# Attention scores in pairs of adjacent PSUM banks: one exponential for two heads, and two of a step's three row maxima by one instruction

## The chip, the cores and the metric

The kernel runs on one core of one Trainium2 chip. The metric is the time of one execution on the device in microseconds (us). The engines are named as in the profile: PE is TensorE (matmuls; PEld are its weight loads), DVE is VectorE, ACT is ScalarE, POOL is GpSimd and SP is SyncE, which issues the DMAs. PSUM, the memory that PE writes its sums to, has eight banks; one bank holds 512 float32 numbers in each of 128 partitions.

## What is computed

Two attention blocks read the same input x of 2048 rows and 448 columns, and a gate mixes their results. Both blocks have 16 heads of 28 columns. Block A is local: each row looks at 8 rows at a distance of 2. Block B is full attention, and its 2048 x 2048 scores for each head are most of the work.

```python
def _B_ref(x, wqkv, wo):
    ...
    q, k, v = qkv[0], qkv[1], qkv[2]
    scores = jnp.einsum("bhqd,bhkd->bhqk", q, k) * (Dh ** -0.5)
    p = _softmax(scores, axis=-1)
    o = jnp.einsum("bhqk,bhkd->bhqd", p, v)
    return (lambda x, *d: x.transpose(*d))(o, 0, 2, 1, 3).reshape(B, S, D) @ wo

x = A_x
g = _sigmoid((x * gate_w).sum(-1, keepdims=True))
a = _A_ref(x, A_wqkv, A_wo)
b = _B_ref(x, B_wqkv, B_wo)
return g * a + (1 - g) * b
```

## The kernel before

All products are taken in two parts: a number is split into a high part and a low remainder, and a product is the sum of high x high, low x high and high x low. So a score block needs three matmuls (0, 1 and 2 below).

**PSUM.** Four single banks `R[0]` to `R[3]` (L52) stand for the whole kernel. The other four are first one tile `T[0]` of four banks (L60), and after the projections three single banks `T[0]` to `T[2]` (L445) and one for the weighted sums, `av` (L443).

**Projections, about the first 284 us.** A list of 92 tiles is worked through: 28 tiles of queries and keys (`qk_tile`, L244), 16 of values (`v_tile`, L262) and 48 for block A (`a_tile`, L268). Each tile is 11 matmuls into one bank (`project`, L241), and the banks rotate over `R[0]` to `R[3]` (`next_bank`). Then the bank is read. The first 11 tiles are read twice, by an ACT copy (L248, the high part) and by a DVE subtraction (L254, the low part). The later query and key tiles are read by two ACT copies (L248, L251) and subtracted on POOL. The tiles of values and of block A are read by one ACT copy (L265, L275). From the twelfth tile on, a *quad* follows each tile: four matmuls of the *first pass* (L121) into the four banks of `T[0]`, and one DVE maximum over all four (L125). The first pass computes scores with the high parts alone, to get the row maxima that the softmax subtracts later. It has 1024 blocks in all, and 80 quads take 320 of them.

**The step loop.** Block B is 16 units (four groups of four heads, times four blocks of 512 queries) of 16 steps each; a step `kt` takes 128 keys for four heads. In a step, `scores` (L862) issues 12 score matmuls (L882), three for each of four heads, and four exponentials on ACT (L885), one for each head's bank. In the order of PE stand also three blocks of the first pass, for units that come later: s0, s1 and s2, each a matmul (L121) with its own DVE maximum (L125). The order is written out in the string `WITH`: "10" is head 1, part 0; a head's exponential follows its part 2. After the scores come four products with the values (L851, `do_av`) for the step *before*. The 704 blocks that the quads leave last for 235 steps, so the last 21 steps run without s0 to s2, in the order `ALONE`. The seven banks rotate (L888-889): what a step's scores, exponentials and maxima free is handed out in a fixed order to the next step. Block A's work, and the steps by which a finished unit is scaled and stored, lie between, on POOL, DVE and ACT, where a small planner puts them: it counts a step as 2.3 us and a maximum as 0.607 us of DVE, and issues block A's instructions for DVE while its count is not behind.

**The output projection.** It starts in the last 21 steps. Seven of its instructions are issued after a step's products (`op_some`, L911). Row block j collects in one of two banks, `accs[j % 2]`, by matmuls at L693; then ACT copies the bank out (`op_out`, L701, for j up to 7; `op_part`, L809, for j = 8 to 11). `side["t"]` and `side["f"]` are banks for transposes. After the last step, j = 8 to 11 get their last products in four banks and a DVE addition each (`op_rest`, L814), and j = 12 to 15 are computed in the four banks of `order`.

Of the kernel before, what the change touches and what calls it, by code (L numbers as in the profile page):

```python
# [8 lines left out]
F32 = mybir.dt.float32  # L9
F32R = mybir.dt.float32r  # L10
AF = mybir.ActivationFunctionType
# [8 lines left out]
SCALE = DH ** -0.5  # L20
# [5 lines left out]
def gated_mix_kernel(ctx: ExitStack, tc: tile.TileContext, xT, xn, gw, wA, wB, woAB, out):  # L26
    nc = tc.nc
# [18 lines left out]
    pp = ctx.enter_context(tc.tile_pool(name="pp", bufs=16))  # L46
# [25 lines left out]
    KH = [cp.tile([128, S], F32R, name=f"KH{i}") for i in range(2)]  # L72
    KL = [cp.tile([128, S], F32R, name="KL0")]
# [4 lines left out]
    def init_kh(t):  # L78
        nc.gpsimd.memset(t.bitcast(F32), 1.0)

    def ptile(name):
        return pp.tile([128, 512], F32, tag="P", name=name)

    def dma_r(dst, src):
        nc.sync.dma_start(dst.bitcast(F32), src.bitcast(F32))  # L85
# [29 lines left out]
    def s1_mm(n, bank):  # L115
        u, i = divmod(n, 64)
        qs, kc, h = i // 16, i // 4 % 4, i % 4
        if i == 0 and u + 1 < NU:
            qhis[u + 1] = load_part(u + 1, "qhi", qk_hi)
        r = slice(32 * h, 32 * h + DH)  # L120
        nc.tensor.matmul(bank, qhis[u][r, 128 * qs:128 * qs + 128],  # L121
                         KH[u // NB % 3][r, 512 * kc:512 * kc + 512], start=True, stop=True)

    def s1_max(n, k, bank):
        nc.vector.tensor_reduce(MX[:, n % NMX:n % NMX + k], bank, axis=X, op=ALU.max)  # L125
        if n // 64 != (n + k) // 64:
            finished.append(n // 64)
        s1c[0] = n + k
# [28 lines left out]
            nc.sync.dma_start(nm[u].bitcast(F32)[:, 32 * a:32 * a + 32], r[32 * a:32 * a + 32, :])  # L157


    t0 = ptile("t0")  # L160
    nc.vector.memset(t0, 0.0)
    nc.vector.memset(zt, 0.0)
    nc.vector.memset(omg, 0.0)
# [2 lines left out]
    with tc.tile_pool(name="xp", bufs=1) as xp, tc.tile_pool(name="wp", bufs=2) as wp:  # L166
# [57 lines left out]

        banks4 = R
        pn = [0]
# [93 lines left out]
        r, t = xst[:, 0, 0:3, :], xst[:, 0, 3, :]  # L320
# [40 lines left out]
        for n, t in enumerate(tiles):  # L361
# [37 lines left out]
            if parts:  # L399
                u, t = parts.pop(0)  # L400
# [165 lines left out]
    for c in range(8):  # L566
# [20 lines left out]
        n = 0  # L587
# [10 lines left out]
    late = {"pool": 0.0, "dve": 0.0}  # L598
# [181 lines left out]
    for u in range(NU - 1):  # L780
        f = NJ * (u + 1)
# [72 lines left out]

    WITH = "10 20 s0 11 21 00 30 12 22 31 01 s1 32 02 s2".split()
    ALONE = "00 10 20 30 01 11 21 31 02 12 22 32".split()
    held = {}
    order = R + T  # L860

    def scores(u, kt, cur):  # L862
        g = u // NB
        n = s1c[0]
        k = min(3, s1e - n)
        qh, ql = Qs[u]
        ks = slice(128 * kt, 128 * kt + 128)
        free = list(order)
        for tok in WITH if k else ALONE:
            if tok[0] == "s":  # L870
                i = int(tok[1])
                held[tok] = free.pop(0)
# [7 lines left out]
            if t == 0:  # L880
                held[a] = free.pop(0)
            nc.tensor.matmul(held[a], (KH[g % 3], KH[g % 3], KL[g % 2])[t][r, ks], (qh, ql, qh)[t][r, :], start=(t == 0), stop=(t == 2))  # L882
            if t == 2:
                p = ptile("P")
                nc.scalar.activation(p, held[a], AF.Exp, scale=SCALE)  # L885
# [25 lines left out]
    for u in range(NU):  # L911
        g, b = divmod(u, NB)
        for kt in range(NJ):
            st = NJ * u + kt
            now[0] = st
            if kt == 12 and u + 1 < NU:
                load_q(u + 1)
            run("pre", st)
            issue("sp", st, 0)
            if st >= A_START:  # L920
                issue("pool", st, 4.2)
            if not adone and not any(lists.values()) and st > stored[0]:
                a_done(st)
            cur = {}
            left = s1e - s1c[0]
            for a in scores(u, kt, cur):
                if a == 2:
                    run("mid", st)
            run("dve", st)
            if u and kt == 6:  # L930
                late["dve"] += 0.25
            if finished:
                v = finished.pop(0)
                t = max_parts(v)
# [39 lines left out]
    for j in range(12, 16):  # L974
# [4 lines left out]
        bank = acc[j - 12]  # L979
# [40 lines left out]
```

## Time and profile before

| what | value |
|---|---|
| time, median of 3 runs | 959.87 us (958.42 to 961.14) |
| the profiled execution, its own time | 962.09 us |
| its span in the profile | 960.3 us |
| granted TensorE clock | 0.996 |
| PE busy | 947.0 us (99%) |
| DVE busy | 746.2 us (78%) |
| ACT busy | 647.7 us (67%) |
| POOL busy | 521.9 us (54%) |

In rows of the timeline the first number is the start in us from the start of the span, the second the length; then engine, line of the kernel, operation, output and input with their shapes, and how many such instructions the row joins. In brackets stands how long the engine was idle before, and what ended it. In rows of groups the numbers behind the first bar are the busy time in us and the mean length of one in ns, and behind the second the idle time before them.

### The profile page before, as it was taken

How to read it: one execution, taken by the hardware profiler on the slowest of the kernel's cores; microseconds unless marked ns; L12 is line 12 of the kernel's file. 1: busy time of each engine (PE TensorE's matmuls, PEld its weight loads, DVE VectorE, ACT ScalarE, POOL GpSimd, SP SyncE). 2: the span in 40 equal slices, each digit the busy share in tenths (PEclk: the TensorE clock that was granted, in tenths of full speed). 3: DMA queues.
4: the chain of work that ended last, by engine and by line, in shares of the span. 5: the costliest groups of instructions: out<-in, count | busy, mean ns of one | idle time of the engine just before them, and what ended most of it. 6: DMA issues, size and time to landing. Idle time of an engine off the chain costs nothing.

```text
span 960.3 us, 19993 instructions
## 1 busy us (share of the span) xinstructions
PE 947.0 (99%) x7578; PEld 553.0 (58%) x7578; DVE 746.2 (78%) x1166; ACT 647.7 (67%) x1309; POOL 521.9 (54%) x384
## 2 busy tenths in 40 slices
PE   8999999999999999999999999999999999999988
PEld 6766777777764544445444444444444444465657
DVE  6477888887779999999999999999998888400012
ACT  4434212122139999999999999999999999856541
POOL 1346101010018689999999999999993853100000
PEclk9999999999999999999999999999999999999999
DMA  9868414354246241314515331520312123344332
GB/s 277 284 199 251 137 48 126 108 135 127 77 117 212 67 126 50 89 47 118 157 42 124 108 88 37 167 72 22 107 43 51 33 68 111 111 141 127 110 102 90
DMA packets 102392, 108.15 MB, mean 113 GB/s; under 512 B 60844, under 2 KB 72636, under 8 KB 101400
## 3 DMA queue, kind: packets, MB, share of 16 engines
q1 hardware_dynamic: 102152, 106.62, 38.4%
q8 instruction: 59, 0.97, 0.4%
q10 hardware_dynamic: 144, 0.26, 0.1%
q14 instruction: 37, 0.30, 0.1%
HBM read 65.89 MB, written 40.48 MB: 111 GB/s over the span
## 4 chain that ended last, share of the span: by engine, by line
PE 87%; DMA 5%; DVE 3%; POOL 2%; SPq 1%; ACT 1%; issue 1%; ACTq 0%; DVEq 0%
PE av L851 25%; PE r L241 19%; PE r L882 15%; PE T L882 11%; PE T L121 6%; PE r L693 4%; PE T L693 4%; PE r L121 3%; DVE MX L125 2%; DMA kt<-a_scr 1%; DMA oal<-oa_scr 1%; PE r L671 1%; SPq L85 1%; POOL prod L541 1%; POOL oat L546 1%
## 5 line engine op out<-in xcount | busy, mean ns | idle before, releaser
L125 DVE TENSOR_REDUCE MX<-T 128x1 f32<-128x512 f32 (+1 forms) x384 | 384.6, 1021 | 59.6 <-PE T L121 54.5
L885 ACT ACTIVATE P<-r 128x512 f32<-128x512 f32 x581 | 329.8, 609 | 53.6 <-PE r L882 32.5
L125 DVE TENSOR_REDUCE MX<-r 128x1 f32<-128x512 f32 x400 | 262.5, 686 | 22.4 <-PE r L121 16.5
L851 PE MATMUL av<-P,V 128*32 128x512 f32 x2048 | 273.6, 606 | 0.4 <-ACT osb L708 0.4
L885 ACT ACTIVATE P<-T 128x512 f32<-128x512 f32 x443 | 255.7, 610 | 19.8 <-PE r L882 11.1
L121 PE MATMUL T<-KH,qhi 28*128 28x512 f32 x624 | 169.9, 475 | 0.9 <-DVE MX L125 0.6
L882 PE MATMUL r<-QH,KH 30*128 30x512 f32 x581 | 166.5, 471 | 1.2 <-ACT ast L275 0.6
L121 PE MATMUL r<-KH,qhi 28*128 28x512 f32 x400 | 162.6, 455 | 0.0
L882 PEld LDWEIGHTS r<-QH,KH 30*128 30x128 f32 x581 | 75.4, 183 | 125.5 <-DVE MX L125 111.3
L882 PE MATMUL T<-QH,KH 30*128 30x512 f32 x443 | 146.2, 472 | 1.0 <-ACT P L885 0.5
L882 PE MATMUL r<-QL,KH 28*128 28x512 f32 x581 | 141.8, 394 | 0.0
L882 PE MATMUL r<-QH,KL 28*128 28x512 f32 x581 | 141.4, 392 | 0.0
L491 POOL TENSOR_TENSOR prod<-qt,kt 128x896 f32<-128x896 f32 x64 | 135.0, 2114 | 7.1 <-DMA kt<-a_scr 7.0
L882 PE MATMUL T<-QL,KH 28*128 28x512 f32 x443 | 120.6, 395 | 0.0
L882 PE MATMUL T<-QH,KL 28*128 28x512 f32 x443 | 119.9, 392 | 0.0
L546 POOL TENSOR_TENSOR oat<-oat,prod 128x896 f32<-128x896 f32 x56 | 118.1, 2110 | 2.4
L882 PEld LDWEIGHTS T<-QH,KH 30*128 30x128 f32 x443 | 59.8, 182 | 91.5 <-DVE MX L125 86.5
L275 ACT ACTIVATE ast<-r 128x448 f32<-128x448 f32 x48 | 26.1, 545 | 106.7 <-PE r L241 102.3
L541 POOL TENSOR_TENSOR prod<-vt,L 128x896 f32<-128x896 f32 x56 | 95.5, 1705 | 0.7
L121 PEld LDWEIGHTS T<-KH,qhi 28*128 28x128 f32 x624 | 70.9, 182 | 35.9 <-DVE MX L125 27.6
L851 PEld LDWEIGHTS av<-P,V 128*32 128x32 f32 x2048 | 40.3, 108 | 67.6 <-issue 62.1
L681 DVE TENSOR_TENSOR oalo<-r,oah 128x384 fp32r<-128x384 f32 x16 | 8.9, 558 | 90.3 <-ACT onhi L680 80.6
(127 smaller groups left out, 1438.8 us busy)
## 6 DMA issues: line engine op xcount, KB each, us to landing
a_scr<-ast SPq DMA_DIRECT2D x24, 448.0 KB
qk_hi<-qkh SPq DMA_DIRECT2D x24, 256.0 KB
qk_lo<-qkl SPq DMA_DIRECT2D x24, 256.0 KB
rbc<-rs SPq DMA_DIRECT2D x60, 64.0 KB
KH<-qk_hi SPq DMA_DIRECT2D x16, 224.0 KB
qhi<-qk_hi SPq DMA_DIRECT2D x64, 56.0 KB
xg<-in_xn SPq DMA_DIRECT2D x16, 224.0 KB
KL<-qk_lo SPq DMA_DIRECT2D x16, 224.0 KB
```

Of the source, the lines that this page charges most:

```text
L85: nc.sync.dma_start(dst.bitcast(F32), src.bitcast(F32))
L121: nc.tensor.matmul(bank, qhis[u][r, 128 * qs:128 * qs + 128], KH[u // NB % 3][r, 512 * kc:512 * kc + 512], start=True, stop=True)
L125: nc.vector.tensor_reduce(MX[:, n % NMX:n % NMX + k], bank, axis=X, op=ALU.max)
L241: nc.tensor.matmul(bank, wa if wfirst else xa, xa if wfirst else wa, start=(i == 0), stop=(i == len(ORDER) - 1))
L275: nc.scalar.activation(stage[0][:, :, j % 2, :], bank[:, :D].rearrange("p (c e) -> p c e", e=56), AF.Copy)
L491: nc.gpsimd.tensor_tensor(out=p, in0=qt[c], in1=kvt["k", c % 2][:, HALO - DIL * w:HALO - DIL * w + NJ, :], op=ALU.mult)
L541: nc.gpsimd.tensor_tensor(out=dst.rearrange("p j (h d) -> p j h d", d=DH), in0=kvt["v", c % 2][:, HALO - DIL * w:HALO - DIL * w + NJ, :].r ...
L546: nc.gpsimd.tensor_tensor(out=oat[c], in0=oat[c], in1=oat[c, w], op=ALU.add)
L693: nc.tensor.matmul(bank[:, :D], src, wo[c][:, k, :], start=(first and k == ks[0] and i == 0), stop=(last and k == ks[-1] and i == 2))
L851: nc.tensor.matmul(av[32 * h:32 * h + 32, :], V[:, kt, 4 * g + h, :], tiles_[h], start=(kt == 0), stop=(kt == NJ - 1), skip_group_check=True)
L882: nc.tensor.matmul(held[a], (KH[g % 3], KH[g % 3], KL[g % 2])[t][r, ks], (qh, ql, qh)[t][r, :], start=(t == 0), stop=(t == 2))
L885: nc.scalar.activation(p, held[a], AF.Exp, scale=SCALE)
```

## The change

- `R` is no longer four tiles of one bank but the halves of two tiles of two adjacent banks, `RP[0]` and `RP[1]`. `R[0]` and `R[1]` are the halves of `RP[0]`, `R[2]` and `R[3]` those of `RP[1]`. The projections still rotate over `R[0]` to `R[3]`.
- The three banks `T` become one tile of two banks, `T[0]`, and one single bank, `T[1]`.
- In a step, heads "1" and "2" are always in `RP[0]`, and heads "3" and "0" in a pair that alternates from step to step between `RP[1]` and `T[0]` (`mine`); s1 and s2 go to the other one of these two (`other`), s0 to `T[1]`.
- An exponential covers a pair, 1024 columns: one follows "22", one follows "02". The maximum of s0 is taken alone, those of s1 and s2 by one instruction over a pair.
- The orders `WITH` and `ALONE` are changed to suit: s1 and s2 now stand last.
- The tiles for exponentials and other buffers in SBUF come from a pool of 8 pairs instead of 16 singles; single buffers are handed out as halves.
- The planner counts a step as 2.25 us and a maximum as 0.58 us.
- In the output projection, the two banks of `accs` are the halves of one pair, `side["f"]` is the second of them, `side["t"]` is `T[1]`, and `order` is the two halves of `RP[0]` and those of the remaining pair.

```diff
-    R = [ps.tile([128, 512], F32, name=f"r{i}") for i in range(4)]
+    RP = [ps.tile([128, 2, 512], F32, name=f"r{i}") for i in range(2)]
+    R = [t[:, i, :] for t in RP for i in range(2)]
...
-    banks([(), (), ()], ctx)
+    banks([(2,), ()], ctx)
...
     def s1_close():
-        order[:] = [held[x] for x in "0123"]
-        rest = [t for t in T + R if all(t is not o for o in order)]
-        accs.extend(rest[0:2])
-        side["f"], side["t"] = rest[1:3]
+        accs.extend(sums(1 - turn[0]))
+        side["f"], side["t"] = accs[1], T[1]
+        order.extend([RP[0][:, 0, :], RP[0][:, 1, :], *sums(turn[0])])
...
-    WITH = "10 20 s0 11 21 00 30 12 22 31 01 s1 32 02 s2".split()
+    WITH = "10 20 s0 11 21 30 00 12 22 31 01 32 02 s1 s2".split()
...
+        mine, other = ((RP[1], T[0]) if turn[0] == 0 else (T[0], RP[1]))
+        if k:
+            turn[0] = 1 - turn[0]
+        bank = {"1": RP[0][:, 0, :], "2": RP[0][:, 1, :], "3": mine[:, 0, :], "0": mine[:, 1, :],
+                "s0": T[1], "s1": other[:, 0, :], "s2": other[:, 1, :]}
...
                 if i < k:
-                    s1_mm(n + i, held[tok])
-                    s1_max(n + i, 1, held[tok])
+                    s1_mm(n + i, bank[tok])
+                if i == 0:
+                    s1_max(n, 1, T[1])
+                elif i == 2 and k > 1:
+                    s1_max(n + 1, k - 1, other[:, 0:k - 1, :])
...
-            if t == 2:
-                p = ptile("P")
-                nc.scalar.activation(p, held[a], AF.Exp, scale=SCALE)
-                cur[h] = p
+            if t == 2 and a in "20":
+                p = pair("P")
+                nc.scalar.activation(p, RP[0] if a == "2" else mine, AF.Exp, scale=SCALE)
+                cur[(h + 3) % 4], cur[h] = p[:, 0, :], p[:, 1, :]
                 yield len(cur)
-        if k:
-            order[:] = [held[x] for x in ("s0", "1", "s1", "2", "s2", "3", "0")]
...
-            step = 2.3 if left else 2.1
-            late["dve"] = max(0.0, late["dve"] + 0.607 * min(3, left) - step)
+            step = 2.25 if left else 2.1
+            late["dve"] = max(0.0, late["dve"] + 0.58 * min(3, left) - step)
```

The instructions of the engines are in program order, and a row in brackets waits for the engine that it names; instructions of one kind that follow one another are joined. First PE in the projections, at tiles of block A. Before, `r_128` to `r_131` are the four single banks, `T_0` is the tile of the quads, and L241 are a tile's 11 matmuls:

```order
L241 MATMUL r_129<-wh_1333,xh_175 128x448 [waits Activation_49]
L241 MATMUL r_129<-wh_1333,xh_175 128x448 x3
L241 MATMUL r_129<-wl_1334,xh_175 128x448 x4
L241 MATMUL r_129<-wh_1333,xl_179 128x448 x3
L121 MATMUL T_0_135<-KH_146,qhi 128x512 [waits DVE_49]
L121 MATMUL T_0_135<-KH_146,qhi 128x512 x3
L241 MATMUL r_130<-wh_1333,xh_175 128x448 [waits Activation_49]
L241 MATMUL r_130<-wh_1333,xh_175 128x448 x3
L241 MATMUL r_130<-wl_1334,xh_175 128x448 x4
L241 MATMUL r_130<-wh_1333,xl_179 128x448 x3
```

After, at the same place, `r_128` and `r_129` are the two pairs, and these are the two halves of `r_129` (lines are shifted: L241 is now L250, L121 is L130):

```order
L250 MATMUL r_129<-wh_1622,xh_171 128x448 x4
L250 MATMUL r_129<-wl_1623,xh_171 128x448 x4
L250 MATMUL r_129<-wh_1622,xl_175 128x448 x3
L130 MATMUL T_0_133<-KH_145,qhi 128x512 [waits DVE_49]
L130 MATMUL T_0_133<-KH_145,qhi 128x512 x3
L250 MATMUL r_129<-wh_1622,xh_171 128x448 [waits Activation_49]
L250 MATMUL r_129<-wh_1622,xh_171 128x448 x3
L250 MATMUL r_129<-wl_1623,xh_171 128x448 x4
L250 MATMUL r_129<-wh_1622,xl_175 128x448 x3
```

Before, every tile's first matmul waits for the ACT copy that last read its bank, which is that of four tiles earlier. After, a tile in a first half has no wait of its own, and a tile in a second half waits for the copy of the tile just ahead of it, in the first half of the same pair: the wait goes by the tile of PSUM, and the pair is now one.

Second, PE at the turn from one step to the next. Before, from s1 to the next step's "30" (L882 are scores, L121 s0 to s2, L851 the products with the values):

```order
L121 MATMUL r_131<-KH_147,qhi 128x512 [waits Activation_49]
L882 MATMUL r_129<-QH,KL_148 128x512
L882 MATMUL r_130<-QH,KL_148 128x512
L121 MATMUL r_128<-KH_147,qhi 128x512 [waits Activation_49]
L851 MATMUL av<-P,V 32x512 x4
L882 MATMUL T_2_2299<-QH,KH_146 128x512 [waits DVE_49]
L882 MATMUL T_0_2297<-QH,KH_146 128x512 [waits Activation_49]
L121 MATMUL r_131<-KH_147,qhi 128x512 [waits DVE_49]
L882 MATMUL T_2_2299<-QL,KH_146 128x512
L882 MATMUL T_0_2297<-QL,KH_146 128x512
L882 MATMUL T_1_2298<-QH,KH_146 128x512 [waits Activation_49]
L882 MATMUL r_128<-QH,KH_146 128x512 [waits DVE_49]
```

After, from s1 to the next step's "22" (`r_128` is `RP[0]`, `r_129` is `RP[1]`, `T_0` the other pair, `T_1` the bank of s0; L898 are scores, L130 s0 to s2, L859 the products):

```order
L130 MATMUL T_0_2239<-KH_2244,qhi 128x512 [waits Activation_49]
L130 MATMUL T_0_2239<-KH_2244,qhi 128x512
L859 MATMUL av<-P,V 32x512 x4
L898 MATMUL r_128<-QH,KH_145 128x512 [waits Activation_49]
L898 MATMUL r_128<-QH,KH_145 128x512
L130 MATMUL T_1_2240<-KH_2244,qhi 128x512 [waits DVE_49]
L898 MATMUL r_128<-QL,KH_145 128x512 x2
L898 MATMUL T_0_2239<-QH,KH_145 128x512 [waits DVE_49]
L898 MATMUL T_0_2239<-QH,KH_145 128x512
L898 MATMUL r_128<-QH,KL_2245 128x512 x2
```

Before, s1 and s2 each wait for one exponential of the step before, and "30" for the maximum of s2 of the step before. After, s1 waits for the exponential of the whole pair in which the step before had heads "3" and "0", and "30" and "00" for the one maximum over s1 and s2 in that same pair.

Third, PE in the output projection, where row block j = 0 ends and j = 1 begins (L693, now L702). Before:

```order
L693 MATMUL T_2_2299<-wo_10261,onhi_10791 128x448 [waits DMAHW6_49]
L693 MATMUL T_2_2299<-wo_10262,onhi_10791 128x448 [waits Pool_49]
L693 MATMUL T_2_2299<-wo_10261,onlo_10792 128x448 [waits DMAHW7_49]
L693 MATMUL r_128<-wo_10261,oah 128x448 [waits Activation_49]
L693 MATMUL r_128<-wo_10262,oah 128x448
```

After:

```order
L702 MATMUL r_129<-wo_9117,onhi_9572 128x448 [waits DMAHW6_49]
L702 MATMUL r_129<-wo_9118,onhi_9572 128x448 [waits Pool_49]
L702 MATMUL r_129<-wo_9117,onlo_9573 128x448 [waits DMAHW7_49]
L702 MATMUL r_129<-wo_9117,oah 128x448 [waits Activation_49]
L702 MATMUL r_129<-wo_9118,oah 128x448
```

Before, the two row blocks are in different tiles, and the wait of j = 1 is for an earlier reader of its own bank and for its input; after, both are in `r_129`, and j = 1 waits for the ACT copy that reads j = 0.

More of the change, by code (lines that the diff above doesn't have):

```diff
@@ L45, in gated_mix_kernel @@
     sp = ctx.enter_context(tc.tile_pool(name="sp", bufs=2))
-    pp = ctx.enter_context(tc.tile_pool(name="pp", bufs=16))
+    pp = ctx.enter_context(tc.tile_pool(name="pp", bufs=8))
     ps = ctx.enter_context(tc.tile_pool(name="ps", bufs=1, space=bass.MemoryType.PSUM))
-    R = [ps.tile([128, 512], F32, name=f"r{i}") for i in range(4)]
+    RP = [ps.tile([128, 2, 512], F32, name=f"r{i}") for i in range(2)]
+    R = [t[:, i, :] for t in RP for i in range(2)]
     tctx = [ExitStack()]
@@ L79, in init_kh, with pair @@
         nc.gpsimd.memset(t.bitcast(F32), 1.0)
+    def pair(name):
+        return pp.tile([128, 2, 512], F32, tag="P", name=name)
+    half = []
     def ptile(name):
-        return pp.tile([128, 512], F32, tag="P", name=name)
+        if not half:
+            t = pair(name)
+            half.extend((t[:, 1, :], t[:, 0, :]))
+        return half.pop()
     def dma_r(dst, src):
@@ L157, in max_store @@
             nc.sync.dma_start(nm[u].bitcast(F32)[:, 32 * a:32 * a + 32], r[32 * a:32 * a + 32, :])
-    t0 = ptile("t0")
+    t0 = pair("t0")[:, 0, :]
     nc.vector.memset(t0, 0.0)
@@ L852, in do_av, with sums @@
                              start=(kt == 0), stop=(kt == NJ - 1), skip_group_check=True)
-    WITH = "10 20 s0 11 21 00 30 12 22 31 01 s1 32 02 s2".split()
-    ALONE = "00 10 20 30 01 11 21 31 02 12 22 32".split()
-    held = {}
-    order = R + T
+    WITH = "10 20 s0 11 21 30 00 12 22 31 01 32 02 s1 s2".split()
+    ALONE = "10 20 30 00 11 21 31 01 12 22 32 02".split()
+    turn = [0]
+    order = []
+    def sums(i):
+        t = T[0] if i else RP[1]
+        return t[:, 0, :], t[:, 1, :]
     def scores(u, kt, cur):
@@ L867, in scores @@
         ks = slice(128 * kt, 128 * kt + 128)
-        free = list(order)
+        mine, other = ((RP[1], T[0]) if turn[0] == 0 else (T[0], RP[1]))
[3 more added lines that the diff above has]
+                "s0": T[1], "s1": other[:, 0, :], "s2": other[:, 1, :]}
         for tok in WITH if k else ALONE:
@@ L871, in scores @@
                 i = int(tok[1])
-                held[tok] = free.pop(0)
                 if i < k:
-                    s1_mm(n + i, held[tok])
-                    s1_max(n + i, 1, held[tok])
+                    s1_mm(n + i, bank[tok])
[3 more added lines that the diff above has]
+                    s1_max(n + 1, k - 1, other[:, 0:k - 1, :])
                 continue
@@ L879, in scores @@
             r = slice(32 * h, 32 * h + (DH + 2 if t == 0 else DH))
-            if t == 0:
-                held[a] = free.pop(0)
-            nc.tensor.matmul(held[a], (KH[g % 3], KH[g % 3], KL[g % 2])[t][r, ks], (qh, ql, qh)[t][r, :], start=(t == 0), stop=(t == 2))
-            if t == 2:
-                p = ptile("P")
-                nc.scalar.activation(p, held[a], AF.Exp, scale=SCALE)
-                cur[h] = p
+            nc.tensor.matmul(bank[a], (KH[g % 3], KH[g % 3], KL[g % 2])[t][r, ks], (qh, ql, qh)[t][r, :], start=(t == 0), stop=(t == 2))
+            if t == 2 and a in "20":
+                p = pair("P")
+                nc.scalar.activation(p, RP[0] if a == "2" else mine, AF.Exp, scale=SCALE)
+                cur[(h + 3) % 4], cur[h] = p[:, 0, :], p[:, 1, :]
                 yield len(cur)
-        if k:
-            order[:] = [held[x] for x in ("s0", "1", "s1", "2", "s2", "3", "0")]
     opj = [0]
```

## Prediction

> **What bounds the kernel now.** I read the page first (which engine is busy), then the busy time by stretches, then the timeline of one stretch in each stage, because a busy PE says nothing about which loop sets its pace.
>
> ```profile
> PE 947.0 (99%) x7578; PEld 553.0 (58%) x7578; DVE 746.2 (78%) x1166; ACT 647.7 (67%) x1309; POOL 521.9 (54%) x384
> 322.00:692.00 370.00, 369.51 (x3677) 179.18 (x3669) 357.41 (x693) 341.28 (x683) 352.75 (x240) 1.00 0.33 91
> ```
>
> The second line is a stretch of the step loop; its columns after the length are PE, PEld, DVE, ACT and POOL. PE is filled, but DVE (357.41 of 370) and ACT (341.28) are nearly so too. Hence no engine has much room, and what a step takes is set by the loops between them. The step length comes from the copies of `av`, one in each unit of 16 steps:
>
> ```profile
> 730.42 0.66 ACT L708 ACTIVATE osb<-av 128x512 f32<-128x512 f32 x1
> 767.33 0.63 ACT L708 ACTIVATE osb<-av 128x512 f32<-128x512 f32 x1
> ```
>
> 36.91 / 16 = 2.307 us a step. The loop that gives it stands in one step of the timeline (L882 scores, L885 exponentials, the L121 load is s2, L851 the products):
>
> ```profile
> 734.51 0.50 PE L882 MATMUL r<-QH,KH 30*128 30x512 f32 x2
> ...
> 735.11 1.32 DVE L125 TENSOR_REDUCE MX<-r 128x1 f32<-128x512 f32 x2 [0.46 <-PE r L121]
> ...
> 735.57 1.08 ACT L885 ACTIVATE P<-r 128x512 f32<-128x512 f32 x2 [0.32 <-PE T L882]
> ...
> 736.34 0.68 DVE L125 TENSOR_REDUCE MX<-T 128x1 f32<-128x512 f32 x1
> 736.54 1.10 ACT L885 ACTIVATE P<-T 128x512 f32<-128x512 f32 x2
> ...
> 737.08 0.18 PEld L882 LDWEIGHTS T<-QH,KH 30*128 30x128 f32 x1
> ...
> 737.69 0.18 PEld L121 LDWEIGHTS T<-KH,qhi 28*128 28x128 f32 x1
> ...
> 737.78 1.08 ACT L885 ACTIVATE P<-r 128x512 f32<-128x512 f32 x2
> ...
> 738.11 0.16 PEld L851 LDWEIGHTS av<-P,V 128*32 128x32 f32 x8 [0.24 <-issue]
> ...
> 739.10 0.18 PEld L882 LDWEIGHTS r<-QH,KH 30*128 30x128 f32 x2 [0.84 <-DVE MX L125]
> ```
>
> A step starts at 734.51. Its first exponential starts 1.06 later and the fourth ends at 736.54 + 1.10 = 737.64, 2.07 after the first began. The *next* step's s2 needs the bank of that fourth exponential and loads at 737.69, 0.05 later. The products start 0.42 behind it, and the step after that 0.99 later, at 739.10. So two steps take 1.06 + 2.07 + 0.05 + 0.42 + 0.99 = 4.59, or 2.295 each: this loop from PE over ACT to PE makes the 2.307. DVE holds "30" the same way: the third maximum ends at 737.02 and the load of "30" is at 737.08.
>
> **Part 1: exponentials and maxima in pairs.** The prices of the wider instructions come from shapes that are there:
>
> ```profile
> L125 DVE TENSOR_REDUCE MX<-r 128x1 f32<-128x512 f32 x400 | 262.5, 686 | 22.4 <-PE r L121 16.5 <-PE r L882 3.0 <-PE T L882 1.6
> L125 DVE TENSOR_REDUCE MX<-T 128x4 f32<-128x2048 f32 x80 | 183.3, 2292 | 45.0 <-PE T L121 44.1
> L275 ACT ACTIVATE ast<-r 128x448 f32<-128x448 f32 x48 | 26.1, 545 | 106.7 <-PE r L241 102.3 <-issue 4.4
> L248 ACT ACTIVATE qkh<-r 128x512 fp32r<-128x512 f32 x28 | 16.7, 597 | 44.5 <-PE r L241 44.5
> L885 ACT ACTIVATE P<-r 128x512 f32<-128x512 f32 x581 | 329.8, 609 | 53.6 <-PE r L882 32.5 <-PE T L882 17.7
> ```
>
> A maximum over 512 columns takes 0.686, one over 2048 takes 2.292, so 512 columns more cost 0.535, and the pair takes 1.22 in place of two of 0.686. On ACT, 64 columns more cost 597 - 545 = 52 ns, that is 0.81 ns a column, and an exponential over 1024 would take 0.609 + 512 x 0.81 ns = 1.02. Two overlap: the rows above show 735.57 to 736.54, 0.97 for two, against 2 x 0.609, so 0.12 each. Two pairs then take 2 x 1.02 - 0.12 = 1.92 or 1.93 in place of 2.07. Bounds: at worst a pair costs what two singles do now (2.07); at best the columns alone count, 2048 x 0.81 ns, and the fixed part (609 - 415 = 194 ns) once, 1.85. I take 1.93, which rests on the rows with the same kind of read.
>
> By the Trainium skill (ScalarE: Activation LUTs, What ACT_TABLE_LOAD costs) an ACTIVATE with immediate scale and bias takes 186 ns + 0.833 ns a column and neighbours overlap by about 93 ns; that is an estimate of 1.985 for the two, and the loop below would be 2.31 instead of 2.28, 7 us more in all. Its 612 ns for 512 columns agrees with the 609 of the row.
>
> What is late next? The old loop becomes 1.06 + 1.93 + 0.05 + 0.42 + 0.99 = 4.45, or 2.225. But the order is changed too. s1 and s2 both go into the pair of the step before's *last* exponential, the maximum over them starts only when both are there, and "30", which waits for it, now stands ahead of "12" and "22", so the first exponential is behind it as well. This loop, from the end of the second exponential to that of two steps later, is: 0.05 to the load of s1; 0.60 from load to maximum (734.51 to 735.11 for s0); 1.22 for the pair; 0.06 to "30"; 0.70 from "30" to the exponential (737.08 to 737.78); 1.93. In all 4.56, or 2.28 a step. The gain of the exponentials is thus mostly given back: 2.295 to 2.28 is 0.015 in each of 235 steps, **-3.5 us**. Bounds: the old loop's 2.225 (-16) if "30" finds its maximum done, and with exponentials at 2.07 2.35 (+13). The planner's numbers only move block A's work, and I cost them at nothing; DVE's spare time, 12.6 in 370, covers it, and it grows by 2 x 0.686 - 1.22 = 0.15 a step at most.
>
> **Part 2: the halves of a pair hold each other.** The order in the changed program shows what the diff doesn't say: a projection tile in a second half now waits for the reader of the first half, which holds the tile just before it. That reader was never in the way, since banks came round after four tiles. PE works in order, so all that is queued behind (quads, tiles) waits too. The first tiles are held by the DVE subtraction:
>
> ```profile
> 13.10 1.54 PE L241 MATMUL r<-xh,wh 128*128 128x512 f32 x4
> 15.35 0.69 DVE L254 TENSOR_TENSOR qkl<-r,qkh 128x512 fp32r<-128x512 f32 x1
> 16.09 1.07 PE L241 MATMUL r<-xh,wh 128*128 128x512 f32 x4
> 18.59 1.07 PE L241 MATMUL r<-xh,wh 128*128 128x512 f32 x4
> 19.42 0.69 DVE L254 TENSOR_TENSOR qkl<-r,qkh 128x512 fp32r<-128x512 f32 x1 [1.80 <-ACT qkh L248]
> ```
>
> Tile 3 starts at 18.59; the reader of tile 2 ends at 19.42 + 0.69 = 20.11, and with 0.05 it is 1.57 late. Tiles 3, 5, 7, 9 and 11 are alike: 7.9. Tile 1 would go from 13.10 to 16.09, 2.99, of which 0.5 is its own delay now (2.99 against 16.09 to 18.59, 2.50), so 2.5. Sum **10.4**. The later query and key tiles are held by the second ACT copy, those of values and block A by their one copy:
>
> ```profile
> 52.24 0.77 PEld L241 LDWEIGHTS r<-xh,wh 128*128 128x128 f32 x4 [0.24 <-issue]
> ...
> 52.41 0.59 ACT L251 ACTIVATE qkr<-r 128x512 f32<-128x512 f32 x1
> ```
>
> ```profile
> 157.79 0.55 ACT L275 ACTIVATE ast<-r 128x448 f32<-128x448 f32 x1 [2.26 <-PE r L241]
> 158.16 0.70 PEld L241 LDWEIGHTS r<-wh,xh 128*128 128x128 f32 x4 [0.25 <-issue]
> ...
> 158.29 2.29 DVE L125 TENSOR_REDUCE MX<-T 128x4 f32<-128x2048 f32 x1 [0.61 <-PE T L121]
> ...
> 160.63 0.19 PEld L121 LDWEIGHTS T<-KH,qhi 28*128 28x128 f32 x4 [0.32 <-DVE MX L125]
> ```
>
> In the first, 52.41 + 0.59 + 0.05 - 52.24 = 0.81, for 8 tiles (13 to 27, every other): **6.5**. In the second, 157.79 + 0.55 + 0.05 - 158.16 = 0.23, for 32 tiles: 7.4; but the next quad waits for DVE anyway (158.29 + 2.29 = 160.58, quad at 160.63), which can cover some or, at worst for my sum, all of it. I take **6**, as the tile fills the time to that quad.
>
> The output projection has the same in `accs`: j + 1 waits for the copy that reads j, where the other bank had been free.
>
> ```profile
> 841.28 0.57 PE L693 MATMUL r<-wo,oah 128*128 128x448 f32 x2
> 841.48 0.55 ACT L701 ACTIVATE res<-T 128x448 f32<-128x448 f32 x1 [0.91 <-PE T L693]
> ...
> 850.03 0.68 PE L693 MATMUL T<-wo,oah 128*128 128x448 f32 x2
> ...
> 851.05 0.58 ACT L701 ACTIVATE res<-r 128x448 f32<-128x448 f32 x1
> ...
> 928.62 0.57 ACT L809 ACTIVATE part<-T 128x448 f32<-128x448 f32 x1
> ```
>
> First of eleven: 841.48 + 0.55 + 0.05 - 841.28 = 0.80; the second, where exponentials stand ahead of the copy, 1.65. The eleven sum to **10.1**, all on PE, which nothing else holds here. In the tail it is four waits, the first and the last pair of rows:
>
> ```profile
> 934.31 0.67 PE L693 MATMUL r<-wo,onhi 128*128 128x448 f32 x2
> 934.33 0.62 DVE L814 TENSOR_TENSOR res<-T,part 128x448 f32<-128x448 f32 x1 [2.81 <-PE T L693]
> ...
> 954.56 0.57 PE L693 MATMUL T<-wo,onhi 128*128 128x448 f32 x2
> ...
> 954.76 0.55 ACT L701 ACTIVATE res<-r 128x448 f32<-128x448 f32 x1 [7.26 <-PE r L693]
> ```
>
> 934.33 + 0.62 + 0.05 - 934.31 = 0.69, and 954.76 + 0.55 + 0.05 - 954.56 = 0.80; four of about 0.8 are **3.2**.
>
> **Sum.** 10.4 + 6.5 + 6 + 10.1 + 3.2 - 3.5 = +32.7. The profiled execution took 962.09, so the changed one 994.8; the profiled one lies 2.2 above the median of 959.87, which gives **992.6**, said as 992.
>
> **Rivals.** *Faster: the halves don't hold each other.* If two banks of one tile can be written and read at once, and the waits that I read in the order are for older readers, part 2 is nothing and only the steps remain: -3.5 to -16, 956 to 944, say 953. For it: they are different banks, and before, neighbours never met. Against it: the waits stand on exactly every second tile, and the first-half tiles have none. Chance 0.07. The Trainium skill (PSUM — Partial Sum Buffer, PSUM bank collisions raise a hardware error) asks for a guard by bank and quadrant of partitions; by that rule the second half would need no wait, and this rival would hold. No row of before shows a pair, so the trace doesn't decide it.
>
> *Slower still: the steps get longer.* If s2 can only load behind s1, a load later (0.18, as at 737.69), the maximum over both and "30" are late by that in each turn of the loop: (4.56 + 0.18) / 2 = 2.37, which is 0.075 more than 2.295, 235 x 0.075 = +17.6 in place of -3.5, so 1014. The loop is a loss from a sum of 4.59 on, that is, from 0.03 of such lateness. For it: s1 and s2 are last, right behind "02". Against it: they work on different rows of the array. Chance 0.13, half of it below 1010.
>
> *No change: the steps gain as much as the halves cost.* They would have to fall to about 2.14 (235 x 0.154 = 36.2, the sum of part 2), 960. PE's 369.51 of 370 speaks against it, and so do both loops. Chance 0.05.
>
> **The numbers.** The forecast has 0.75. Its own range goes from 974 (steps 2.225, 12.5 better, and the 6 of values and block A covered) to 1009 (steps 2.35, 16.5 worse). With the part of the longer steps that lies next to it, and a little for halves that are covered elsewhere, the range is 970 to 1010; outside are the faster rival, no change and half of the still slower, 0.19 in all. A measurement can tell about 0.3% here, 3 us. Faster 0.07, within it 0.05, slower 0.88.
>
> **What would show it.** Right: in the projections every second tile starts 0.05 behind the reader of the tile before it, and the step loop begins some 23 us later than before; the copies of `av` are some 36.5 to 36.7 apart; an output block starts behind the copy of the one before. Wrong: tiles that start while the other half of their pair is read (the faster rival); copies of `av` 35.6 apart or less, or over 37.6 (the loop of s1, s2 and "30" is priced wrongly); exponentials over 1024 that take other than about 1.02; a time below 970.

## The result, and the profile after

The changed kernel takes 1022.63 us (median of 4 runs, 1020.45 to 1023.48) where the kernel before takes 960.08 beside it: a ratio of 1.065, with a 95% interval of 1.0627 to 1.0673. The forecast was 992, with a range up to 1010. The direction was right and the size was not: +62.6 in place of +32.7, so I looked for a second cause as large as the first.

The page of the changed kernel, its line of busy times:

```profile
PE 970.4 (95%) x7578; PEld 518.9 (51%) x7578; DVE 737.4 (72%) x932; ACT 619.7 (61%) x797; POOL 521.9 (51%) x384
```

ACT and DVE have less to do, as they should (ACT 647.7 before, DVE 746.2), and PE's busy share falls from 99% to 95%: PE waits. Where it waits shows when the profiled executions (1020.45 and 962.09) are cut at four places that both traces have: the first load of the step loop's scores, the first step without s0 to s2, the start of the last step, and the end. The rows that give the first two cuts, those of the kernel before first:

```profile
280.81 0.18 PEld L882 LDWEIGHTS r<-QH,KH 30*128 30x128 f32 x2 [1.01 <-ACT ast L275]
...
828.79 0.18 PEld L882 LDWEIGHTS r<-QH,KH 30*128 30x128 f32 x1 [0.66 <-ACT P L885]
```

```profile
309.14 0.18 PEld L898 LDWEIGHTS r<-QH,KH 30*128 30x128 f32 x2 [1.01 <-ACT ast L284]
...
874.86 0.18 PEld L898 LDWEIGHTS r<-QH,KH 30*128 30x128 f32 x2 [0.20 <-issue]
```

| stage, us | before | after | difference | forecast |
|---|---|---|---|---|
| projections, to the first scores | 280.8 | 309.1 | +28.3 | +22.9 |
| 235 steps with s0 to s2 | 548.0 | 565.7 | +17.7 | -3.5 |
| the next steps, to the start of the last | 96.8 | 103.4 | +6.6 | +10.1 |
| the last step and the tail | 34.7 | 40.4 | +5.7 | +3.2 |
| span | 960.3 | 1018.7 | +58.4 | +32.7 |

Three stages came out within 5.4 us of their terms, two above and one below, so that these misses partly cancel (+4.4 together). The step loop, which was to gain 3.5, lost 17.7: 21 of the 26 us that the forecast lacks are there. In a unit of 16 steps the copies of `av` are 38.47 apart, 2.404 a step:

```profile
619.57 0.61 ACT L717 ACTIVATE osb<-av 128x512 f32<-128x512 f32 x1
...
658.04 0.60 ACT L717 ACTIVATE osb<-av 128x512 f32<-128x512 f32 x1
```

The wide instructions cost what the forecast took from other shapes, 1.02 for an exponential over 1024 columns and 1.22 for a maximum over a pair:

```profile
L901 ACT ACTIVATE P<-r 128x1024 f32<-128x1024 f32 x374 | 370.5, 1024 | 121.6 <-PE r L898 93.1 <-PE T L898 27.4 <-ACT nmv L155 0.3
L134 DVE TENSOR_REDUCE MX<-r 128x2 f32<-128x1024 f32 x117 | 143.3, 1225 | 26.5 <-PE T L898 25.6 <-ACT osb L717 0.4 <-PE r L130 0.3
```

So the prices are right, and a loop is wrong. The second row has the clue: the pair maximum over s1 and s2 (L130) is, by the profile's account, released in 25.6 of its 26.5 us of waiting not by their matmuls but by those of the scores (L898). One step of the changed kernel, from the load of "30" to that of the next "30":

```profile
821.84 0.19 PEld L898 LDWEIGHTS T<-QH,KH 30*128 30x128 f32 x2 [0.21 <-DVE MX L134]
...
822.05 0.19 PEld L130 LDWEIGHTS r<-KH,qhi 28*128 28x128 f32 x2
...
822.18 0.40 PE L898 MATMUL T<-QL,KH 28*128 28x512 f32 x2
...
822.41 0.40 PE L898 MATMUL T<-QH,KL 28*128 28x512 f32 x2
...
822.97 1.23 DVE L134 TENSOR_REDUCE MX<-r 128x2 f32<-128x1024 f32 x1 [0.36 <-PE T L898]
...
824.25 0.19 PEld L898 LDWEIGHTS r<-QH,KH 30*128 30x128 f32 x2 [0.20 <-DVE MX L134]
```

"30" loads at 821.84. "31" and "01" start at 822.18, "32" and "02" at 822.41, 0.57 behind "30". s1 and s2 load at 822.05, long before, but the maximum starts at 822.97, 0.56 behind the start of "02", which stands ahead of s1 and s2 in PE's order. It ends at 824.20, and the next "30" loads at 824.25. That is a loop of *one* step: 0.57 + 0.56 + 1.23 + 0.05 = 2.41. No exponential is in it.

### The profile page after: what moved, and what is told of

It reads as the page before. It is cut to its first block, busy times and chain, and to the rows that moved or that the text cites. A ratio compares the mean times of both kernels' runs of the same rounds, so it can differ in the third digit from the quotient of the medians.

```text
span 1018.7 us, 19535 instructions
## 1 busy us (share of the span) xinstructions
PE 970.4 (95%) x7578; PEld 518.9 (51%) x7578; DVE 737.4 (72%) x932; ACT 619.7 (61%) x797; POOL 521.9 (51%) x384
## 4 chain that ended last, share of the span: by engine, by line
PE 82%; ACT 4%; issue 2%; DMA 1%; POOL 1%; SPq 0%; DVE 0%; ACTq 0%; POOLq 0%; DVEq 0%
PE r L898 25%; PE av L859 24%; PE r L250 15%; PE T L898 9%; PE r L702 6%; PE T L130 2%; ACT ast L284 1%; ACT P L901 1%; DMA raw<-in_wA 1%; PE T L702 1%; PE T L680 1%; ACT res L710 0%; SPq L94 0%; ACT V L274 0%; POOL wl L184 0%
## 5 line engine op out<-in xcount | busy, mean ns | idle before, releaser
L134 DVE TENSOR_REDUCE MX<-T 128x1 f32<-128x512 f32 (+2 forms) x433 | 487.7, 1127 | 98.5 <-PE T L130 62.5
L901 ACT ACTIVATE P<-r 128x1024 f32<-128x1024 f32 x374 | 370.5, 1024 | 121.6 <-PE r L898 93.1
L859 PE MATMUL av<-P,V 128*32 128x512 f32 x2048 | 272.7, 605 | 0.2 <-ACT osb L717 0.2
L130 PE MATMUL T<-KH,qhi 28*128 28x512 f32 x790 | 203.6, 464 | 0.1
L898 PE MATMUL r<-QH,KH 30*128 30x512 f32 x748 | 185.8, 495 | 1.9 <-ACT P L901 1.2
L898 PEld LDWEIGHTS r<-QH,KH 30*128 30x128 f32 x748 | 69.1, 181 | 230.3 <-ACT P L901 200.0
L134 DVE TENSOR_REDUCE MX<-r 128x2 f32<-128x1024 f32 x117 | 143.3, 1225 | 26.5 <-PE T L898 25.6
L898 PE MATMUL r<-QH,KL 28*128 28x512 f32 x748 | 159.6, 422 | 0.0
L898 PE MATMUL r<-QL,KH 28*128 28x512 f32 x748 | 148.0, 392 | 0.0
L901 ACT ACTIVATE P<-T 128x1024 f32<-128x1024 f32 x138 | 140.8, 1020 | 0.0
L130 PEld LDWEIGHTS T<-KH,qhi 28*128 28x128 f32 x790 | 79.7, 181 | 26.4 <-DVE MX L134 21.3
L859 PEld LDWEIGHTS av<-P,V 128*32 128x32 f32 x2048 | 40.3, 108 | 93.8 <-issue 88.5
L250 PE MATMUL r<-wh,xh 128*128 128x448 f32 x256 | 69.3, 392 | 8.9 <-ACT ast L284 5.0
L898 PE MATMUL T<-QH,KH 30*128 30x512 f32 x276 | 68.8, 494 | 1.9 <-ACT P L901 1.8
L898 PEld LDWEIGHTS r<-QL,KH 28*128 28x128 f32 x748 | 70.3, 184 | 0.0
L898 PEld LDWEIGHTS r<-QH,KL 28*128 28x128 f32 x748 | 69.9, 183 | 0.8
```

What stands on the lines that cost most here:

```text
L250: nc.tensor.matmul(bank, wa if wfirst else xa, xa if wfirst else wa, start=(i == 0), stop=(i == len(ORDER) - 1))
L859: nc.tensor.matmul(av[32 * h:32 * h + 32, :], V[:, kt, 4 * g + h, :], tiles_[h], start=(kt == 0), stop=(kt == NJ - 1), skip_group_check=True)
L898: nc.tensor.matmul(bank[a], (KH[g % 3], KH[g % 3], KL[g % 2])[t][r, ks], (qh, ql, qh)[t][r, :], start=(t == 0), stop=(t == 2))
L901: nc.scalar.activation(p, RP[0] if a == "2" else mine, AF.Exp, scale=SCALE)
```

## The experiments

All but the last three are edits of the changed kernel, in one place each (the one for the halves at the end in two); each was timed in three rounds beside the kernel before on the same chip. Which stage moved is read from the same four cuts as above.

**The order of s1 and s2.**

```diff
-    WITH = "10 20 s0 11 21 30 00 12 22 31 01 32 02 s1 s2".split()
+    WITH = "10 20 s0 11 21 30 00 12 22 31 01 s1 s2 32 02".split()
```

> The changed kernel with one edit: in the order WITH, s1 and s2 stand ahead of "32" and "02" instead of behind them. Theory (one-step loop): in the changed kernel's steps "30" waits for the pair maximum, the maximum starts 0.54 us after the last matmul ahead of it in PE's order, which is "02", and the next "30" waits for that maximum: 0.58 (from "30" to "02") + 0.54 + 1.23 + 0.05 = 2.40 a step. Then the maximum starts a round (0.24) earlier, this loop falls to 2.16, and another one takes over (ScalarE: s1 still waits for the exponential of the step before, and "32" and "02" are now behind it, 2.29 to 2.40): 996 to 1022. Rival (the forecast's two-step loop over the first exponential): the way from "30" to the first exponential is unchanged, no change, 1022.

Measured: 998.2, ratio to the kernel before 1.0381 (1.0354 to 1.0407); the 235 steps take 540.3 in place of 565.7, the other stages within 3 us. A step of it, where "30" loads at 790.49 and the pair maximum starts at 791.37:

```profile
790.49 0.18 PEld L898 LDWEIGHTS T<-QH,KH 30*128 30x128 f32 x2
...
790.84 0.41 PE L130 MATMUL r<-KH,qhi 28*128 28x512 f32 x2
...
791.06 0.39 PE L898 MATMUL T<-QH,KL 28*128 28x512 f32 x2
...
791.37 1.23 DVE L134 TENSOR_REDUCE MX<-r 128x2 f32<-128x1024 f32 x1
```

The maximum starts 0.31 behind "02" (791.06), where it was 0.56: it no longer waits for it. The rival, that the order of s1 and s2 doesn't matter, is out.

**How often the maximum counts.** A loop of one step and one of two steps differ in what a shorter maximum is worth.

```diff
-                    s1_max(n + 1, k - 1, other[:, 0:k - 1, :])
+                    s1_max(n + 1, k - 1, other[:, 0:k - 1, 0:448])
```

> The changed kernel, with the pair maximum over s1 and s2 taken over 448 of each bank's 512 columns (the last 64 of each are left out of the row maxima). The instruction gets 128 x 1.046 ns = 0.134 us shorter, and nothing else changes. Theory (one-step loop through the maximum): each of 235 steps gets 0.134 shorter, 2.40 to 2.27, that is -31 us, 991. Rival (the forecast's two-step loop): half of that a step, -16 us, 1007. Second rival (TensorE has no room, the maximum is hidden): 1022.

Measured: 993.39, ratio 1.0321 (1.0289 to 1.0352). The copies of `av`:

```profile
604.03 0.60 ACT L717 ACTIVATE osb<-av 128x512 f32<-128x512 f32 x1
...
640.37 0.61 ACT L717 ACTIVATE osb<-av 128x512 f32<-128x512 f32 x1
```

The maximum itself, 1225 ns long before this edit:

```profile
L134 DVE TENSOR_REDUCE MX<-r 128x2 f32<-128x896 f32 x117 | 127.7, 1092 | 19.5 <-PE T L898 17.3 <-PE r L130 1.8
```

36.34 / 16 = 2.271, against 2.404: in this unit each step got 0.133 shorter for an instruction 0.133 shorter. Over all 235 steps it is 29.8 us (535.9 in place of 565.7), of the 31 expected. A loop over two steps would have given half. This is the one-step loop.

**The halves in the projections.**

```diff
-    R = [t[:, i, :] for t in RP for i in range(2)]
+    R = [t[:, i, :] for i in range(2) for t in RP]
```

> The changed kernel with R in another order: first halves of both pairs, then the second halves, so that a projection tile shares its pair with the tile two before it and not with the one just before. Theory (halves of a pair hold each other): all waits of the second halves are over before they are reached, the step loop starts 28 us earlier, at 281 as in the kernel before, and the time is 994 to 996. Rival (the projections are late for another reason, as the pool of pair buffers in SBUF): no change, 1022.

Measured: 995.1, ratio 1.0351 (1.0326 to 1.0377). The first scores load at 281.91, 27.2 earlier, and the steps take 566.9 as before:

```profile
281.91 0.18 PEld L898 LDWEIGHTS r<-QH,KH 30*128 30x128 f32 x2 [1.01 <-ACT ast L284]
```

**Exponentials in fours.**

```diff
-                nc.scalar.activation(p, RP[0] if a == "2" else mine, AF.Exp, scale=SCALE)
+                for i in range(2):
+                    nc.scalar.activation(p[:, i, :], (RP[0] if a == "2" else mine)[:, i, :], AF.Exp, scale=SCALE)
```

> The changed kernel with the exponentials in fours again: each pair's exponential is two instructions of 512 columns, back to back, at the place of the one of 1024. ScalarE needs some 0.14 us more a step. Theory (one-step loop through the maximum, ScalarE not in it): its own loop is 2.30 to 2.37 then, still under 2.40: no change, 1022 (+-4). Rival (the forecast's loop, with the exponentials in it): 0.07 a step more, +16, 1039.

Measured: 1008.48, ratio 1.0485 (1.046 to 1.0511). Neither expectation held: with more work on ACT the kernel got 14 us *faster*, all in the steps (552.0 in place of 565.7). The view of the maximum's line shows what had changed beside ACT. In the changed kernel:

```profile
L134 DVEq EVENT_SEMAPHORE  x233: 21/21/21, 312.8 to 871.0; - x117
```

and with the exponentials in fours:

```profile
L134 DVEq EVENT_SEMAPHORE  x1: 21/21/21, 311.1 to 311.1; - x1
```

In the changed kernel the pair maximum waits for two engines, and the program puts one of the two waits, that for PE, into an instruction of its own ahead of it; the maximum itself keeps the wait for ACT. This second wait is for the exponential of the step before that read this pair, which was over long ago; s1 had waited for it already. Yet because of it the maximum comes behind the instruction that waits for PE: in the step shown above that instruction starts at 822.903, and the maximum 0.064 later. With four exponentials the second wait is gone. The order of DVE, in the changed kernel and with this edit:

```
L134 TENSOR_REDUCE MX<-T_0_2239 128x2 [waits PE_49,Activation_49]
L134 TENSOR_REDUCE MX<-T_0_2239 128x2 [waits PE_49]
```

The step of this run:

```profile
790.26 0.50 PE L898 MATMUL r<-QH,KH 30*128 30x512 f32 x2
...
790.84 0.40 PE L898 MATMUL r<-QH,KL 28*128 28x512 f32 x2
...
791.32 1.23 DVE L134 TENSOR_REDUCE MX<-T 128x2 f32<-128x1024 f32 x1 [0.23 <-PE r L898]
...
792.61 0.18 PEld L898 LDWEIGHTS T<-QH,KH 30*128 30x128 f32 x2 [0.15 <-DVE MX L134]
```

0.58 from "30" to "02" as before, but 0.48 from "02" to the maximum in place of 0.56, and a step of 2.34 (37.42 between two copies of `av`). The 0.064 a step that the copies show, 235 times, is 15 us.

**One exponential of the two in halves**, to tell the second wait from the shorter exponentials; the second wait is still there, 233 times in the same view.

```diff
-                nc.scalar.activation(p, RP[0] if a == "2" else mine, AF.Exp, scale=SCALE)
+                src = RP[0] if a == "2" else mine
+                for c in ((0, 1), (1, 2)) if a == "0" else ((0, 2),):
+                    nc.scalar.activation(p[:, c[0]:c[1], :], src[:, c[0]:c[1], :], AF.Exp, scale=SCALE)
```

> The changed kernel with only the second exponential of a step (heads "3" and "0") as two of 512 columns; the first stays one of 1024. In the run with both split, the time fell by 14 us, and the pair maximum, which waits for TensorE and ScalarE in the changed kernel (the first of the two waits as an instruction of its own, 0.064 us ahead of the maximum), waited for TensorE alone. Here both waits are kept. Theory (the second wait costs 0.064 in the one-step loop, 235 x 0.064 = 15 us): nothing gained, 1022 (+-4), with steps of 2.40. Rival (exponentials of 512 free their banks earlier): some or all of the 14 us here too, 1008 to 1015.

Measured: 1025.19, ratio 1.0645 (1.061 to 1.068), steps 566.2: nothing gained. A kernel with both exponentials in halves *and* the second wait, or with neither, wasn't tried; that the 14 us are the second wait's rests on this run and on the links of the step above, in which only the one from "02" to the maximum got shorter.

**The halves at the end.** Some lines of the edit; the projections' `R` gets a pool of its own that is closed after them, and `RP[1]` is allocated last, so that its pool can be closed when the first pass ends:

```diff
-        accs.extend(sums(1 - turn[0]))
+        assert turn[0] == 1
+        rctx[1].close()
+        pool = ctx.enter_context(tc.tile_pool(name="pa", bufs=1, space=bass.MemoryType.PSUM))
+        accs.extend(pool.tile([128, 512], F32, name=f"acc{i}") for i in range(2))
         side["f"], side["t"] = accs[1], T[1]
-        order.extend([RP[0][:, 0, :], RP[0][:, 1, :], *sums(turn[0])])
+        order.extend([t[:, i, :] for i in range(2) for t in (RP[0], T[0])])
```

> The changed kernel with the pools of PSUM rearranged so that, when the first pass has ended, the free pair is given back and handed out as two single banks for accs; and the four banks of the tail in the order first halves, then second halves. Projections and steps stay in pairs. Theory (halves of a pair hold each other in the output projection and the tail too): the 6.6 us that the last 21 steps and the 5.7 us that the tail grew by go, 1010 to 1014. Rival (they grew because the last steps follow other orders and exponentials of 1024): no change, 1022.

Measured: 1008.09, ratio 1.0476 (1.0446 to 1.0505). The last steps take 95.1 in place of 103.4 and the tail 35.0 in place of 40.4, 13.7 together, where 12.3 was expected, so that the time is some 2 us under the range; the other stages stay.

**The planner's numbers** (2.3 and 0.607 again, nothing else).

```diff
-            step = 2.25 if left else 2.1
-            late["dve"] = max(0.0, late["dve"] + 0.58 * min(3, left) - step)
+            step = 2.3 if left else 2.1
+            late["dve"] = max(0.0, late["dve"] + 0.607 * min(3, left) - step)
```

> The changed kernel with the planner's numbers of the kernel before (2.3 us a step, 0.607 a maximum). Theory (they only move block A's work, which is off the path): no change, 1022 (+-3). Rival (they set when DVE's other work delays a maximum): a few us either way.

Measured: 1024.99, ratio 1.0644 (1.0605 to 1.0683): within the noise they cost nothing here, as forecast.

**All repairs at once:** the interleaved `R`, the order with s1 and s2 ahead of "32" and "02", and `accs` and the tail's banks apart.

> All three repairs at once: R interleaved, s1 and s2 ahead of "32" and "02", accs and the tail's banks apart. If they are independent they add: -27.5 (interleaved) -24.4 (order) -10 (accs and tail) from 1022.6: 960 to 962, what the kernel before takes. If the steps, now bound by ScalarE's loop, gain from the planner's shorter step or lose in the fuller stretches, some us to either side.

Measured: 953.83 (953.61 to 954.4), ratio 0.9911 (0.9887 to 0.9935). It beats the kernel before by 0.9%, and by more than was expected: 960 to 962 counted the repair of `accs` and the tail as 10, and the run above gave 14.5. With that the three add up to 956; the last 2 us stay unexplained. Its stages are 281.2, 540.0, 95.5 and 35.0: what it gains over the kernel before, 8.6, is nearly all in the 235 steps (548.0), so the pairs, with their order and the planner's numbers, are worth 8 us when the waits that they brought are taken away. That is 2.298 a step against 2.332. Its copies of `av` are 36.55 apart in this unit, where the forecast read 36.91 from a unit of the kernel before:

```profile
577.59 0.60 ACT L723 ACTIVATE osb<-av 128x512 f32<-128x512 f32 x1
...
614.14 0.60 ACT L723 ACTIVATE osb<-av 128x512 f32<-128x512 f32 x1
```

**Two more orders for this kernel**, to see what sets its steps now. First "12" and "22" ahead of "30" and "00":

```diff
-    WITH = "10 20 s0 11 21 30 00 12 22 31 01 s1 s2 32 02".split()
+    WITH = "10 20 s0 11 21 12 22 30 00 31 01 s1 s2 32 02".split()
```

> The kernel with all three repairs, and "12" and "22" ahead of "30" and "00" in the order. Theory (after the repairs the steps follow the loop from the second exponential over s1, the products and the next first exponential; the first exponential starts 1.07 after its step in any case, set by "10", "11" and "12"): no gain, since "30" doesn't hold "12" any more: 952 to 956. Rival (the forecast's loop, in which "30" holds the first exponential): some 3% faster steps, 940 or less.

Measured: 953.61, ratio 0.9917 (0.9901 to 0.9934): no change, so "30" doesn't set its steps by way of the first exponential. What does wasn't settled. Then s1 and s2 one place earlier:

```diff
-    WITH = "10 20 s0 11 21 30 00 12 22 31 01 s1 s2 32 02".split()
+    WITH = "10 20 s0 11 21 30 00 12 22 s1 s2 31 01 32 02".split()
```

> The kernel with all three repairs, and s1 and s2 one place earlier still, ahead of "31" and "01". Theory (s1 waits for the second exponential of the step before, to 0.71 after a step's start, and everything behind it in TensorE's order waits too): "31", which started at about 0.55 to 0.57, starts behind 0.71, a round of 0.23 is added between s1 and the products, that is up to 0.12 a step in the two-step loop: 960 to 980. Rival (what matters is only how early the pair maximum starts): the same or faster, 945 to 953.

Measured: 972.32, ratio 1.0108 (1.0088 to 1.0128), steps 558.9. The rows of one step (L131 is s1 and s2, L907 the scores, here "31" and "01"):

```profile
590.86 1.02 ACT L910 ACTIVATE P<-T 128x1024 f32<-128x1024 f32 x1
...
591.93 0.18 PEld L131 LDWEIGHTS T<-KH,qhi 28*128 28x128 f32 x2
591.93 0.19 PEld L907 LDWEIGHTS p<-QL,KH 28*128 28x128 f32 x2
```

s1 loads 0.05 behind the end of the exponential, at 591.88, and "31" right behind s1. So of the three places tried one is good: behind "32" and "02" s1 and s2 hold the maximum, ahead of "31" and "01" their own wait for the exponential holds the scores behind them.

## Why the prediction was wrong, point by point

**The step that failed** is in part 1, in the loop that gave the steps -3.5 us, where they measured +17.7: "This loop, from the end of the second exponential to that of two steps later, is: 0.05 to the load of s1; 0.60 from load to maximum ...". Two things in it were not so. The maximum doesn't start 0.60 behind the load of s1 but 0.92 (822.05 to 822.97), because its semaphore comes in PE's order, behind "32" and "02"; the 0.60 was read from s0, which has nothing late ahead of it. And I closed the loop through the exponentials, over two steps, and never closed the shorter one: "30" holds "32" and "02", these hold the signal of s2, that holds the maximum, and the maximum holds the *next* step's "30". That is 2.40 in one step. The order in the section on the change shows all its links: "30" waits for DVE, and s1 and s2 stand last in the step. The maximum that is 0.133 shorter gave 0.133 a step, which only a loop of one step does. The forecast's own sign of this error, copies of `av` over 37.6 apart, is in the trace: 38.47.

**The second wait** of the pair maximum, 0.064 of the 2.40, stood nowhere in the forecast. The order of DVE has it; the forecast used only PE's. The run without it was 14 us faster.

**The exponentials** were priced right (1.02, two in 1.94 in this trace, forecast 1.93) and were not in the loop, so that their saving did nothing. By the Trainium skill (ScalarE: Activation LUTs, What ACT_TABLE_LOAD costs) two exponentials of 1024 columns were an estimate of 1.985; the trace has 1.94, as this row shows:

```profile
776.46 1.94 ACT L901 ACTIVATE P<-r 128x1024 f32<-128x1024 f32 x2 [0.28 <-PE r L898]
```

**The baseline of the steps** was read from one unit, 2.307. Over all 235 steps the kernel before takes 548.0, 2.332 each; that is why the steps, 2.407 each over all 235, cost 17.7 and not 23.

**The halves in the projections** hold each other just as forecast; one pair of rows for each kind of reader (subtraction, second copy, one copy):

```profile
16.29 0.69 DVE L263 TENSOR_TENSOR qkh<-r,qkh 128x512 fp32r<-128x512 f32 x1
17.03 1.36 PEld L250 LDWEIGHTS r<-xh,wh 128*128 128x128 f32 x4 [3.51 <-DVE qkh L263]
...
58.74 0.59 ACT L260 ACTIVATE qkr<-r 128x512 f32<-128x512 f32 x1
59.38 0.76 PEld L250 LDWEIGHTS r<-xh,wh 128*128 128x128 f32 x4 [1.10 <-ACT qkr L260]
...
165.28 0.55 ACT L284 ACTIVATE ast<-r 128x448 f32<-128x448 f32 x1 [2.14 <-PE r L250]
165.88 0.70 PEld L250 LDWEIGHTS r<-wh,xh 128*128 128x128 f32 x4 [0.43 <-ACT ast L284]
```

Each load starts 0.05 behind the end of the reader: 17.03 behind 16.29 + 0.69 = 16.98, 59.38 behind 59.33, 165.88 behind 165.83. The start of each tile after the change, less its start before it, climbs in stairs, one for each second half. It is 12.7 at tile 12 (forecast 10.4), 19.0 at tile 28 (6.3 more; forecast 6.5) and 28.3 at the end (9.3 more; forecast 6). The first excess is tile 1 and stairs of 1.75 where I had 1.57. The last: stairs of about 0.22, no cover by the quads, and one stair of 2.4 at tile 31, which has a cause that I hadn't thought of:

```profile
122.27 1.04 ACT L183 ACTIVATE wh<-raw 128x448 fp32r<-128x448 f32 x2 [3.56 <-DMA raw<-in_wA]
...
123.22 0.52 ACT L274 ACTIVATE V<-r 128x448 f32<-128x448 f32 x1
...
123.79 0.72 PEld L250 LDWEIGHTS r<-wh,xh 128*128 128x128 f32 x4 [2.65 <-ACT V L274]
```

The copy that holds the tile (L274) was itself queued on ACT behind a split of weights (L183) that waited 3.56 for a DMA. With four single banks the wait for the DMA was about as long, 3.35, but the tile behind didn't depend on that copy:

```profile
102.93 1.05 ACT L174 ACTIVATE wh<-raw 128x448 fp32r<-128x448 f32 x2 [3.35 <-DMA raw<-in_wA]
```

**The end.** The forecast's sum of 10.1 over eleven waits is about 0.8 too high: done again from the rows of before it is 9.3, because row block 8 starts at 905.43, when the copy of block 7 is over (903.68 + 0.55 = 904.23), and has nothing to wait for. With `accs` apart, 8.3 of the last steps went and 5.4 of the tail (forecast 3.2). The last steps then take 1.7 less than before the change, so the pairs gain a little there. The tail differs by 2 to 3 us between runs of kernels that don't touch it (40.1 to 42.9), so its part is not settled closer.

**The rivals.** That halves don't hold each other is out. The Trainium skill's rule (PSUM — Partial Sum Buffer, PSUM bank collisions raise a hardware error) guards by bank and quadrant, and by it second halves needn't wait; here the waits are the program's, set by tile, and the runs don't show what the chip would do without them. The rival of longer steps gave 1014 and was the nearest, but for another reason. Its term for the steps, +17.6, agrees with the measured +17.7 by luck: its condition was that s2 loads behind s1, and they load together (822.05, x2). "No change" needed steps of 2.14, and they took 2.407.

## What to carry to other kernels

When buffers are merged so that one instruction can cover two, ask of every other user of them what now waits for whom: here the fix was to hand the halves out so that neighbours in time lie in different pairs, and that is one line. When a matmul is put last in PE's order, whatever waits for it waits, as here, for all ahead of it; close every loop in the order, the shortest first, and count each for as many steps as it spans. And read the waits on all engines of a loop, since a second wait that is always over can still cost its own time.

## What I had not expected of the hardware

A matmul that started early can signal late: s1 and s2 started at 822.19, before "32" and "02" (822.41), and their maximum started 0.56 behind these. The trace's record of the semaphores says the same: PE's signal for "02" comes at 822.833 and that for s2 behind it, at 822.875, though s2 started 0.2 earlier. When s1 and s2 stood ahead of "32" and "02" in the order, the maximum started 0.31 behind "02", 0.53 behind s1 and s2 themselves (790.84 to 791.37).

```profile
822.19 0.39 PE L130 MATMUL r<-KH,qhi 28*128 28x512 f32 x2
```

And a second wait costs though it was over long before: because of it the other wait became an instruction of its own on DVE (0.021 long in the view of the line), and the maximum started 0.064 behind the start of that instruction. At 235 steps that is 15 us by this figure; the run without it was 14 us faster.
